# The last head of a cached-attention decode block: one accumulator bank cleared earlier, an output projection read in stored order, and small work moved into TensorE's waits

## Chip, cores, metric

One core of a Trainium2 chip runs the whole program. The metric is the device time of one execution in microseconds, as the median of several runs; a profiled run also gives the span (first to last instruction) and the granted TensorE clock.

## The reference

A modulated decode block with one token: a layernorm, attention of 32 query heads over a cache of 8 heads x 32768 keys x 128, an output projection, then a second layernorm and a two-layer ReLU network.

```python
mod = silu(c) @ w_mod                      # sa, ca, ga, sb, cb, gb, 512 each
h = layernorm(x) * (1 + ca) + sa
q = h @ wq                                 # 32 heads of 128
p = softmax(q . k_cache * 128**-0.5)       # 8 cache heads, 4 query heads each
o = p . v_cache
x = x + ga * (o @ wo)                      # wo: 4096 x 512
h = layernorm(x) * (1 + cb) + sb
x = x + gb * (relu(h @ w1) @ w2)           # 512 -> 1792 -> 512
```

The caches are 134 MB in bf16, all weights together 15 MB. Every byte is read once.

## The kernel before

One queue (SyncE) streams everything in a fixed order: w_mod, wq, the heads' K and V alternating, and at the end the last V (in three pieces), wo (four pieces), w1 (two), w2 (six). For each head, VectorE transposes K, TensorE multiplies it with a block-diagonal q (scores), ScalarE takes the exponential, VectorE transposes it, TensorE multiplies with V (`pv`, into `o_ps`, which VectorE must clear first). The order of TensorE's and VectorE's instructions is written by hand. Below, x1 is x after the first addition (`x1T` holds it as columns), hidT are the products with w1, and ffn those with w2. The parts that the change touches:

```python
def open_o(g):                              # clears the bank of head g's o
    o_tiles[g] = ps_o.tile([16, 4 * Dh], F32, tag="o", name="o_ps")
    nc.vector.memset(o_tiles[g][:], 0.0)
# blocks(g): Y <- o_ps, four VectorE steps.     o_cols(g): oT <- Y, TensorE ("column sums")
# normalise(g): oT * Linv, then its spread-out form oA, two VectorE steps; and at a part's end spread(i)
# spread(i): o2 <- oA, one TensorE product and a cast
def project(i):                             # o2 times part i of wo
    ...
    if i < WOROWS:                          # parts 0 and 1 (6 of 8 heads): rows, four strips of the array
        nc.tensor.matmul(
            a_rows[0][32*(r%4):32*(r%4)+1, :].rearrange("o (a ko m) -> o a ko m", a=4, ko=KT),
            lhsT=o2_tiles[i][:, r:r+1],
            rhs=wo_sb[:, r, :].rearrange("p (a m ko) -> p a ko m", a=4, ko=KT), ...)
    ...                                     # parts 2 and 3 (one head each): columns
def join_rows():                            # rows of parts 0 and 1 to columns
    aT = rows_sb("aT")[:, 0, :]
    nc.vector.transpose(out=aT, in_=a_rows[0])
    ...                                     # four small products into attnT_ps
def keep_clock(n): ...                      # n filler products of 128x512, result unused

# the end of the order (head 6 = LAST - 1, head 7 = LAST)
            pv(g, (2,), range(6, 16))
            pv(g, (3,))
            next(soft)                      # sum of the exponentials (TensorE)
            next(soft, None)                # its reciprocal (VectorE)
            open_o(LAST)
            a_rows.append(row_bank("a_ps"))
            blocks(g)
        pv(LAST, (0, 1))
        o_cols(LAST - 1)
        normalise(LAST - 1)                 # with spread(2)
        pv(LAST, (2,))
        pv(LAST, (3,))
        blocks(LAST)
        project(0)
        keep_clock(2)
        o_cols(LAST)
        keep_clock(2)
        normalise(LAST)                     # with spread(3)
        project(1)
        keep_clock(3)
        project(2)
        join_rows()
        keep_clock(4)
        project(3)
        ...                                 # x1T; layernorm between keep_clock(4) and keep_clock(4)
        ...                                 # hidT = w1 products, ReLU on ScalarE to hid_bd
        x1_rows = four_rows(x1T[:], "x1", nc.vector.tensor_copy)
        keep_clock(1)
        ...                                 # 56 ffn products with w2
        o_rows = ffn_ps * gb_rows; o_bf = o_rows + x1_rows      # VectorE, two steps
    nc.scalar.dma_start(out=out..., in_=o_bf[:])
```

## Time and profile before

| | before |
|---|---|
| median of the first 3 runs | 359.49 us (358.87 to 360.19) |
| span of the profiled run, granted clock | 358.0 us, 0.948 |
| HBM read | 149.42 MB, 417 GB/s over the span |
| TensorE, VectorE, ScalarE busy | 79%, 58%, 8% |

The busy shares tell little here: the kernel has a long stage paced by the stream, and a tail of 50 us in which single waits count. The tail is read from the timeline (start us, length us, engine, line, operation, output<-inputs, shapes, count, and in brackets the idle time before it with its releaser, that is, what ended the wait). PE are TensorE's products, PEld its weight loads, DVE is VectorE, ACT ScalarE; SPq and ACTq are the queues from which SyncE and ScalarE issue transfers. These rows of before mark its stages: the column sums of head 7, the first step on x1, the ffn, and the last two steps with the output's issue.

```profile
314.79 0.69 DVE L433 TENSOR_SCALAR_CACHE_REDUCE S_g<-S_ps 128x512 f32<-128x512 f32 x1 [2.92 <-PE S_ps L427]
...
341.85 0.38 PE L526 MATMUL acc_ps<-mask_sb,Y 16*128 16x4 f32 x2
...
346.94 0.16 DVE L690 TENSOR_TENSOR x1T<-acc_ps,modT_sb 128x4 f32<-128x4 f32 x1 [2.10 <-PE acc_ps L574]
...
351.77 3.29 PE L724 MATMUL ffn_ps<-w_sb,hid_bd 128*4 128x128 bf16 x56 [0.25 <-ACT hid_bd L709]
355.10 0.28 DVE L729 TENSOR_TENSOR o_rows<-ffn_ps,gb_rows 4x128 f32<-4x128 f32 x1 [3.26 <-PE ffn_ps L724]
...
355.73 0.55 ACTq L732 DMA_DIRECT2D out_dram<-o_bf  x1
```

The first row, the maximum over the last scores, lies before everything that the change touches. All stages below are given from its start, so that what happened earlier in a run doesn't enter. No wait in these rows names a transfer.

### The profile page before, as it was taken

How to read it: one execution, taken by the hardware profiler on the slowest of the kernel's cores; microseconds unless marked ns; L12 is line 12 of the kernel's file. 1: busy time of each engine (PE TensorE's matmuls, PEld its weight loads, DVE VectorE, ACT ScalarE, POOL GpSimd, SP SyncE). 2: the span in 40 equal slices, each digit the busy share in tenths (PEclk: the TensorE clock that was granted, in tenths of full speed). 3: DMA queues.
4: the chain of work that ended last, by engine and by line, in shares of the span. 5: the costliest groups of instructions: out<-in, count | busy, mean ns of one | idle time of the engine just before them, and what ended most of it. 6: DMA issues, size and time to landing. Idle time of an engine off the chain costs nothing. (4 is left out here: it accounts for less than half of the span.)

```text
span 358.0 us, 4070 instructions
## 1 busy us (share of the span) xinstructions
PE 281.7 (79%) x1351; PEld 114.3 (32%) x1354; DVE 207.7 (58%) x269; ACT 28.2 (8%) x68; POOL 8.5 (2%) x14
## 2 busy tenths in 40 slices
PE   0453681997998798879789798979597979989996
PEld 0121230333343334333333233323233333433445
DVE  8545775784677377463938095826855393832141
ACT  1121003001010101010100100010100010030000
POOL 9000000000000000000000000000000000000000
PEclk9996996799899999999969999999999896999999
DMA  8999999999999999999999999999999999999990
GB/s 324 434 443 432 416 448 425 436 439 421 445 425 432 439 425 445 421 432 436 432 443 423 428 439 429 437 430 421 443 432 432 439 419 443 428 421 428 419 398 14
DMA packets 7077, 149.61 MB, mean 418 GB/s; under 512 B 792, under 2 KB 1048, under 8 KB 2200
## 3 DMA queue, kind: packets, MB, share of 16 engines
q1 hardware_dynamic: 7056, 149.43, 97.3%
q8 instruction: 9, 0.15, 0.1%
q14 instruction: 4, 0.03, 0.0%
q10 hardware_dynamic: 8, 0.00, 0.0%
HBM read 149.42 MB, written 0.00 MB: 417 GB/s over the span
## 5 line engine op out<-in xcount | busy, mean ns | idle before, releaser
L407 DVE STREAM_TRANSPOSE KTt<-Ksb 128x2048 f32<-128x2048 f32 x64 | 143.3, 2284 | 68.5 <-DMA Ksb<-in_A_k_cache_dram 60.7
L489 PE MATMUL o_ps<-Vsb,PT_g 128*16 (+1 forms) x512 | 129.5, 393 | 22.4 <-ACT qbd L391 9.7
L427 PE MATMUL S_ps<-KTt,qbd 128*128 128x512 bf16 x512 | 123.0, 391 | 21.6 <-DVE KTt L407 20.2
L427 PEld LDWEIGHTS <-qbd 128*128 128x128 bf16 x512 | 49.0, 98 | 86.4 <-issue 28.6
L489 PEld LDWEIGHTS o_ps<-Vsb,PT_g 128*16 x416 | 37.2, 89 | 90.2 <-issue 63.9
L433 DVE TENSOR_SCALAR_CACHE_REDUCE S_g<-S_ps 128x512 f32<-128x512 f32 x16 | 11.0, 690 | 28.1 <-PE S_ps L427 28.1
L391 ACT COPY qbd<-qrep_sb 32x128 bf16<-32x128 bf16 x32 | 9.4, 295 | 138.2 <-PE S_ps L427 137.1
L470 DVE STREAM_TRANSPOSE PT_g<-P_g 128x1024 bf16<-128x1024 bf16 x8 | 9.7, 1218 | 6.6 <-ACT P_g L464 6.6
L489 PEld LDWEIGHTS <-PT_g 128*16 128x16 bf16 x96 | 8.4, 90 | 12.1 <-issue 0.8
L461 ACT ACTIVATE nbias<-Mb_ps 128x1 f32<-128x1 f32 x8 | 1.4, 171 | 133.3 <-PE Mb_ps L459 133.3
L233 PE MATMUL xc_ps<-cx_sel,cx_bd 16*128 16x2 bf16 x4 | 0.3, 172 | 12.8 <-DVE cx_bd L227 12.8
L464 ACT ACTIVATE P_g<-S_g,nbias 128x1024 bf16<-128x1024 f32 x8 | 9.2, 1148 | 0.2
L520 DVE SCALAR_TENSOR_TENSOR Y<-o_ps,smask,Y 16x128 f32<-16x128 f32 x24 | 8.1, 339 | 0.8
L179 DVE COPY sel<-ident_bf 128x128 bf16<-128x128 bf16 x4 | 7.6, 3731 | 0.0
L476 PE MATMUL L_ps<-Lexp,ones_f 128*128 128x4 f32 x16 | 3.1, 266 | 4.3 <-DVE Lexp L473 4.3
L518 DVE TENSOR_SCALAR Y<-o_ps,smask 16x128 f32<-16x128 f32 x8 | 2.2, 271 | 6.8 <-PE o_ps L489 6.8
L601 PE MATMUL spare_ps<-qbd,ident_bf 128*128 128x512 bf16 x19 | 5.4, 380 | 0.2 <-issue 0.2
L476 PEld LDWEIGHTS L_ps<-Lexp,ones_f 128*128 128x128 f32 x16 | 3.4, 239 | 6.0 <-issue 5.4
L445 PE MATMUL mT_ps<-ident_f,m_p 128*1 128x128 f32 x8 | 2.2, 270 | 3.9 <-DVE m_p L442 2.0
L539 DVE TENSOR_TENSOR oT_sb<-acc_ps,Linv 128x4 bf16<-128x4 f32 x8 | 1.2, 151 | 6.8 <-PE acc_ps L526 6.8
L448 DVE TENSOR_REDUCE Mrow<-mT_ps 1x4 f32<-1x128 f32 x8 | 2.1, 258 | 4.6 <-PE mT_ps L445 4.6
L510 DVE MEMSET o_ps<- 16x512 f32 x8 | 3.9, 485 | 0.8
(112 smaller groups left out, 86.1 us busy)
## 6 DMA issues: line engine op xcount, KB each, us to landing
Ksb<-in_A_k_cache_dram SPq DMA_DIRECT2D x16, 4096.0 KB, 28.8
Vsb<-in_A_v_cache_dram SPq DMA_DIRECT2D x15, 4096.0 KB, 25.1
wq_sb<-in_A_wq_dram SPq DMA_DIRECT2D x1, 4096.0 KB, 18.9
Vsb<-in_A_v_cache_dram SPq DMA_DIRECT2D x2, 2048.0 KB, 21.6
wm_sb<-in_w_mod_dram SPq DMA_DIRECT2D x1, 3072.0 KB, 10.4
wo_sb<-in_A_wo_dram SPq DMA_DIRECT2D x1, 2048.0 KB, 24.9
w_sb<-in_B_w_dram SPq DMA_DIRECT2D x1, 1344.0 KB
wo_sb<-in_A_wo_dram SPq DMA_DIRECT2D x1, 1024.0 KB, 26.8
```

Source lines behind the costliest of these rows:

```text
L179: nc.vector.tensor_copy(out=sel[:, hp, :].rearrange("p (a c) -> p a c", a=4), in_=src)
L391: nc.scalar.copy(out=o, in_=i)
L407: t = nc.vector.transpose(out=KTt[:].bitcast(F32), in_=Ksb[:, 32 * half:32 * half + 32, :].rearrange("p j d -> p (j d)").bitcast(F32),)
L427: nc.tensor.matmul(S_ps_tiles[g], lhsT=qbd[g % 2][:, hp, s, :], rhs=KTv[:, 16 * sl:16 * sl + 16, h, :, par], start=(t4 == 0 and sl == 0 an ...
L433: nc.vector.tensor_scalar(out=S_tiles[g][:, G, :], in0=S_ps_tiles[g], scalar1=1.0, scalar2=None, op0=ALU.mult, op1=ALU.max, accum_out=m_ti ...
L464: nc.scalar.activation(out=P_g[:], in_=S_g[:].rearrange("p g f -> p (g f)"), func=ACT.Exp, bias=nbias[:], scale=scale, accum_out=l_g[:],)
L470: nc.vector.transpose(out=PT_g[:], in_=P_g[:])
L476: nc.tensor.matmul(L_ps[:], lhsT=ones_f[:], rhs=Lexp[:], start=True, stop=True)
L489: nc.tensor.matmul(o_tiles[g][:], lhsT=PT, rhs=Vx, start=False, stop=False, skip_group_check=True)
L510: nc.vector.memset(o_tiles[g][:], 0.0)
L520: nc.vector.scalar_tensor_tensor(out=Y[:], in0=o[:, s], scalar=smask[:, s:s + 1], in1=Y[:], op0=ALU.mult, op1=ALU.add,)
L601: nc.tensor.matmul(spare[0], lhsT=ident_bf[:], rhs=qbd[0][:, 0, 0:4, :], start=True, stop=True)
```

## The change

The intent is to shorten TensorE's chain between the last head's softmax and the end: (1) clear the last head's o bank a softmax step sooner; (2) move the spread of head 6 to between the products with the third and fourth pieces of V; (3) read wo's rows as stored and let the VectorE transpose do the permutation; (4) put project(1) under head 7's normalisation and drop fillers; (5) compute x1's rows in the layernorm's wait instead of just ahead of the ffn; (6) issue the output from SyncE.

```diff
-def layernorm_T(src_T, stat_in, dst_T, shiftT, nscaleT, tagp):
+def layernorm_T(src_T, stat_in, dst_T, shiftT, nscaleT, tagp, meanwhile=None):
     ...                                        # statistics product, nu
+    if meanwhile:
+        meanwhile()
     ...
 # project, parts 0 and 1
-    a_rows[0][...].rearrange("o (a ko m) -> o a ko m", a=4, ko=KT), lhsT=o2_tiles[i][:, r:r + 1],
-    rhs=wo_sb[:, r, :].rearrange("p (a m ko) -> p a ko m", a=4, ko=KT), ...
+    a_rows[0][...], lhsT=o2_tiles[i][:, r:r + 1],
+    rhs=wo_sb[:, r, :], ...
 # join_rows
-    nc.vector.transpose(out=aT, in_=a_rows[0])
+    nc.vector.transpose(
+        out=aT.rearrange("p (a ko m) -> p a ko m", a=4, ko=KT),
+        in_=a_rows[0].rearrange("p (a m ko) -> p a ko m", a=4, ko=KT),
+    )
 # the order (normalise no longer spreads; in the loop spread follows normalise as before)
+            open_o(LAST)
             pv(g, (2,), range(6, 16))
             pv(g, (3,))
             next(soft)
             next(soft, None)
-            open_o(LAST)
 ...
         pv(LAST, (2,))
+        spread(2)
         pv(LAST, (3,))
 ...
         o_cols(LAST)
         keep_clock(2)
+        project(1)
         normalise(LAST)
-        project(1)
-        keep_clock(3)
+        spread(3)
+        keep_clock(2)
         project(2)
+        keep_clock(1)
         join_rows()
-        keep_clock(4)
+        keep_clock(2)
         project(3)
 ...
-        keep_clock(4)
-        layernorm_T(...)
-        keep_clock(4)
+        keep_clock(3)
+        layernorm_T(..., meanwhile)            # expansion of x1; keep_clock(2); row product; keep_clock(2)
+        x1_rows = const.tile([KT, P], F32)
+        nc.vector.tensor_copy(out=x1_rows[:], in_=x1_ps[0])
 ...
-        x1_rows = four_rows(x1T[:], "x1", nc.vector.tensor_copy)
         keep_clock(1)
 ...
-    nc.scalar.dma_start(out=out..., in_=o_bf[:])
+    nc.sync.dma_start(out=out..., in_=o_bf[:])
```

More of the change, by code (lines that the diff above doesn't have):

```diff
@@ L325, with expand @@
         )
-    def four_rows(src_T, name, copy):
+    def expand(src_T, name):
         e = const.tile([P, 32, KT], F32, name=f"{name}_exp")
@@ L333, in four_rows @@
         )
+        return e
+    def four_rows(e, name):
         r_ps = bank(f"{name}_ps")[0:KT, 0:P]
@@ L337, in four_rows @@
         )
-        rows = const.tile([KT, P], F32, name=f"{name}_rows")
-        copy(out=rows[:], in_=r_ps)
-        return rows
-    gb_rows = four_rows(modT_sb[:, 5 * KT:6 * KT], "gb", nc.scalar.copy)
+        return r_ps
+    gb_rows = const.tile([KT, P], F32)
+    nc.scalar.copy(out=gb_rows[:], in_=four_rows(expand(modT_sb[:, 5 * KT:6 * KT], "gb"), "gb"))
     hT = const.tile([P, KT], BF16)
@@ L545, in normalise @@
         PT_tiles.pop(g)
-        if g == sum(WOP[i]) - 1:
-            spread(i)
     o2_tiles = {}
@@ L568, in project @@
                 nc.tensor.matmul(
-                    a_rows[0][32 * (r % 4):32 * (r % 4) + 1, :].rearrange("o (a ko m) -> o a ko m", a=4, ko=KT), lhsT=o2_tiles[i][:, r:r + 1],
-                    rhs=wo_sb[:, r, :].rearrange("p (a m ko) -> p a ko m", a=4, ko=KT), start=False, stop=(i == WOROWS - 1 and r >= n - 4), skip_group_check=True,
+                    a_rows[0][32 * (r % 4):32 * (r % 4) + 1, :], lhsT=o2_tiles[i][:, r:r + 1],
+                    rhs=wo_sb[:, r, :], start=False, stop=(i == WOROWS - 1 and r >= n - 4), skip_group_check=True,
                 )
@@ L638 @@
                 normalise(g - 1)
+                if g in [sum(w) for w in WOP]:
+                    spread(part_of(g - 1))
             if soft:
@@ L694, with meanwhile @@
         h2T = const.tile([P, KT], BF16)
-        keep_clock(4)
-        layernorm_T(x1T[:], stat2, h2T[:], modT_sb[:, 3 * KT:4 * KT], ncb[:], "ln2")
-        keep_clock(4)
+        x1_ps = []
+        def meanwhile():
+            e = expand(x1T[:], "x1")
+            keep_clock(2)
+            x1_ps.append(four_rows(e, "x1"))
+            keep_clock(2)
+        keep_clock(3)
+        layernorm_T(x1T[:], stat2, h2T[:], modT_sb[:, 3 * KT:4 * KT], ncb[:], "ln2", meanwhile)
+        x1_rows = const.tile([KT, P], F32)
+        nc.vector.tensor_copy(out=x1_rows[:], in_=x1_ps[0])
         for part, (k0, k1) in enumerate(W1P):
@@ L731 @@
         nc.vector.tensor_tensor(out=o_bf[:], in0=o_rows[:], in1=x1_rows[:], op=ALU.add)
-    nc.scalar.dma_start(out=out[0, 0].rearrange("(i n) -> i n", i=KT), in_=o_bf[:])
+    nc.sync.dma_start(out=out[0, 0].rearrange("(i n) -> i n", i=KT), in_=o_bf[:])
 _INS = ['A_x', 'A_k_cache', 'A_v_cache', 'A_wq', 'A_wo', 'B_x', 'B_w1', 'B_w2', 'c', 'w_mod']
```

## The prediction

> **What bounds the kernel now.** I read the occupancy by slices first, then the chain that ended last, then the timeline of the last 60 us, because the diff touches nothing before the last head but a rewritten helper. Occupancy by slices (engine, then 40 digits of 8.95 us each):
>
> ```profile
> PE   0453681997998798879789798979597979989996
> ...
> DMA  8999999999999999999999999999999999999990
> ```
>
> The transfers are saturated until the last slice: 149 MB at 417 GB/s is 358 us by itself, so up to the arrival of the last head's K the stream sets the pace. The table of stretches shows where the stream ends (columns: stretch, PE, PEld, DVE, ACT, POOL, granted clock, share of the DMA engines, GB/s):
>
> ```profile
> 349.00:350.00 1.00, 0.76 (x23) 0.64 (x23) 0.39 (x2) 0.00 (x0) 0.00 (x0) 1.00 0.33 116
> 350.00:351.00 1.00, 1.00 (x39) 0.88 (x37) 0.00 (x0) 0.00 (x0) 0.00 (x0) 1.00 0.01 2
> ```
>
> The data are in at about 349.5 us, but the span ends at 358.0. The end is therefore TensorE's in-order queue with its waits, and the chain names it (start us, length us, what):
>
> ```profile
> 323.25 0.33 PE L_ps L476 x2
> ...
> 323.61 0.18 DVE Linv L479
> ...
> 323.88 0.50 DVE o_ps L510
> ...
> 324.42 7.07 PE o_ps L489 x32
> 331.49 0.33 PE acc_ps L526 x2
> ...
> 332.03 0.30 DVE oA L540
> ...
> 332.38 0.18 PE o_ps L555
> 332.56 6.57 PE o_ps L489 x30
> ...
> 339.56 1.82 PE a_ps L568 x12
> ...
> 341.92 0.31 PE acc_ps L526 x2
> ...
> 342.99 1.00 PE a_ps L568 x8
> ...
> 346.39 0.51 PE acc_ps L574 x16
> ```
>
> The reader is to see three things. TensorE, done with the sum at 323.58, stands until 324.42 because VectorE clears the last head's o only after the reciprocal. It stands again from 331.81 to 332.56, as the spread of head 6 waits for two VectorE steps. And the products with wo's rows are slow for their size, as two rows of the per-line view show (min/median/max ns):
>
> ```profile
> L364 PE MATMUL q_ps<-wq_sb,hT x32: 376/379/380, 21.6 to 23.4; 128*1 128x512 bf16 x32
> ...
> L568 PE MATMUL a_ps<-wo_sb,o_sb x24: 609/630/642, 338.8 to 343.4; 128*1 128x512 bf16 x24
> ```
>
> Both are 1x512 products in four strips of the array; one reads runs of 32 neighbours, the other every fourth element. By the timeline q's last 28 take 1.68 us (0.060 each), wo's 8 at 342.99 take 1.00 us (0.125 each).
>
> **What the Trainium skill says.** "TensorE: Matmul & The Clock Gate", section "Back-to-back issue gap": a warm N=512 matmul costs N/2.4 + 2.5 ns, about 216 ns. The trace has 7.07/32 = 0.221 us: agrees. So keep_clock's fillers cost about 0.22 us each (four take 0.97 us here). "SBUF — State Buffer", section "Door 1: The DMA port swizzle", has a note on 16-byte lines, by which bf16 may be strided up to 8 elements before full bandwidth is lost. A step of 4 elements should then be free; the two rows above say it is not, for four strips at once, and I follow the trace. "DMA: Bandwidth & Descriptors", section "Issuing engines are not separate DMA queues": another issuing engine saves only issue time. The trace has 0.55 us for the output's issue from ScalarE and 0.28 to 0.36 us for the equally small loads from SyncE.
>
> **The change, part by part.** The order of instructions of the built kernels gives each move.
>
> (1) The clearing of o for the last head now stands before the reciprocal, behind Lexp (done at 320.4). It finishes near 321, under head 6's products. The 32 products of head 7 can start at 323.6 instead of 324.42: **-0.84**.
>
> (2) The spread of head 6 moves from before 32 products to between the two 16s. The gap 331.81 to 332.56 (0.75) goes; the spread's own work, 0.1 to 0.18, stays: **-0.6**.
>
> (3) wo's rows are read as stored. At q's rate, 16 products take 0.96 instead of 2.0, and 8 take 0.48 instead of 1.0. For project(0) the path is a race: from the last product of head 7 (339.56) VectorE needs 1.5 us for Y (ready 341.07), while TensorE reaches the column sums only at 341.92, after project(0) and two fillers. Now project(0) and two fillers take 0.96 + 0.44 = 1.4, so Y sets it, at about +1.55 instead of +2.36: **-0.8**.
>
> (4) From the end of those column sums (342.23) to the end of project(3) (346.91) were 4.68 us. New order: two fillers and project(1) 0.44 + 0.48, under which oT and oA (0.54) hide; spread 0.1 to 0.15; two fillers 0.44; project(2) 0.51; one filler 0.22; join 0.17 to 0.2; two fillers 0.44; project(3) 0.51; sum 3.4 to 3.5, so **-1.2**. Of this, about 0.5 is the faster project(1), about 0.45 the wait hidden behind it, and 0.2 or so one filler fewer. Against it: the VectorE transpose of wo's rows, 0.72 us contiguous, now reads PSUM in steps of four. It starts after the cast of o2 (about +1.45) and would end at +2.2, just before join at +2.3, so there is no slack. The start-up shows a penalty for reductions of 128 SBUF elements read with a step: 0.36 against 0.27 us. Scaled to 512 elements (an estimate; that this carries over to PSUM is assumed) it is +0.36, of which 0.25 lands on the path: **+0.25**.
>
> (5) Layernorm: one filler fewer before the statistics (they waited for VectorE until 347.57 anyway), x1's expansion (0.28 on VectorE) lies in the wait from 347.60 to 347.99, and x1's row product (about 0.38) among the four fillers, before h2T at 349.18. I count **0**. After hidT, the row product no longer stands before the first ffn product, which came 0.16 after ScalarE had finished: **-0.14**.
>
> (6) Output issued from SyncE: **-0.2**.
>
> Sum: -0.84 - 0.6 - 0.8 - 1.2 + 0.25 - 0.14 - 0.2 = -3.5. From 359.5: **356.0 us**.
>
> **Rivals.** (a) The transfers become the wait. The last piece of w2 was issued at 341.6 and takes at least 8.8 us, so it lands near 350.4. The first ffn product moves from 351.77 to about 348.4 (the sum without the output), and the last piece's four products of 0.059 us are wanted at about 351.4: 1.0 us to spare. wo's first piece lands at 311.9 + 24.9 = 336.8 and is wanted at 338.1; the third, issued about 312.8, lands near 340.8 and is wanted at about 341.4. All hidden, but with 0.6 to 1.3 us to spare. If one binds, the gain shrinks to about 2.5: 357.0. (b) The strided transpose takes twice as long: join waits some 0.7 more than in my contiguous count, 356.5. (c) The step is not why wo's products are slow: (3) and 0.5 of (4) vanish, gain 2.2: 357.3. Against it stands that the same form runs at 0.060 per product on q, at full clock. (d) Fewer fillers let the clock fall: at half rate the last 10 us cost some 4 more, 360. The granted clock reads 1.00 throughout the tail, and no gap that I foresee is over 0.5 us. Unlikely. A gain of 2% (7.2 us) is out of reach: with the data in at 350.4, then 0.2 of products, 0.6 of VectorE and 2.3 for the output, the span can't fall under about 353.5, which is 4.5 saved.
>
> **Range and chances.** The parts carry plus or minus 0.7 together; the before runs alone spread 358.87 to 360.19. Rivals (a) to (c) lie on the slow side, so the range is 355.1 to 357.8. Within 2% means 352.3 to 366.7: 0.98. Faster 0.01, slower 0.01.
>
> **What would show it.** Step 1: no idle time of TensorE before head 7's first product, VectorE's clear ahead of the reciprocal. Step 2: head 7's second 32 products follow the column sums within 0.1 us. Step 3: wo's row products at 379 ns each, 0.06 apart; column sums released by Y, not by a filler. Step 4: 3.4 to 3.8 us from column sums to the end of project(3); the transpose's mean near 1 us. Step 5: 2.3 us from x1T to the first hidT product as before; ffn starts within 0.1 of ScalarE's end. Step 6: about 2.1 us from o_bf to the end, not 2.3. I am wrong if TensorE is seen to wait for w1, w2 or wo, or if the granted clock falls below 1.00 in the tail.

## The result

| | before | after |
|---|---|---|
| median, 6 runs each | 359.19 us (358.62 to 360.19) | 355.58 us (355.43 to 357.48) |
| ratio, 95% interval | | 0.9906 (0.9881 to 0.9931) |
| span of the profiled run | 358.0 us | 353.7 us |

A ratio is the mean time of one kernel's runs over that of the other's of the same rounds, so it is not quite the ratio of the two medians. The gain is 3.6 us by the medians and 3.4 by the ratio. The two spans differ by more, 4.3 us, and the profile shows why that isn't all the change's doing.

The occupancy by slices of after (same engines as shown of before, one slice is 8.84 us):

```profile
PE   0352781999898979897969797979789787989995
...
DMA  8999999999999999999999999999999999999994
```

The last slice, which for before read 0 in the DMA row, now reads 4: the stream runs into the final slice. The chain that ended last is short, and mostly made of transfers (start us, length us, what):

```profile
305.94 25.65 DMA Vsb<-in_A_v_cache_dram
...
331.61 16.67 DMA w_sb<-in_B_w_dram
...
348.32 2.41 PE ffn_ps L742 x40
...
350.75 0.29 DVE o_rows L747
```

In before the chain went through TensorE's products from 307.6 us on. Here it goes from the ffn back to a landing of w2 at 348.28, and from there to V. The timeline of after has the rows that answer to those of before:

```profile
313.42 0.69 DVE L437 TENSOR_SCALAR_CACHE_REDUCE S_g<-S_ps 128x512 f32<-128x512 f32 x1 [1.99 <-PE S_ps L431]
...
338.27 0.38 PE L530 MATMUL acc_ps<-mask_sb,Y 16*128 16x4 f32 x2
...
340.15 0.61 PEld L576 LDWEIGHTS <-wo_sb 128*128 128x128 bf16 x16 [0.36 <-DMA wo_sb<-in_A_wo_dram]
...
342.33 0.16 DVE L700 TENSOR_TENSOR x1T<-acc_ps,modT_sb 128x4 f32<-128x4 f32 x1 [1.60 <-PE acc_ps L576]
...
348.32 2.39 PE L742 MATMUL ffn_ps<-w_sb,hid_bd 128*4 128x128 bf16 x40 [0.15 <-DMA w_sb<-in_B_w_dram]
350.75 0.28 DVE L747 TENSOR_TENSOR o_rows<-ffn_ps,gb_rows 4x128 f32<-4x128 f32 x1 [5.98 <-PE ffn_ps L742]
```

Two readings. First, waits for transfers (wo, then w2) stand in the tail, which before had none. Second, the maximum over the last scores already starts 1.37 us earlier than in before (313.42 against 314.79), ahead of anything that was changed. The table of stretches explains that (stretch, PE, PEld, DVE, ACT, POOL busy, granted clock, DMA share, GB/s); before, then after:

```profile
296.00:298.00 2.00, 2.00 (x7) 0.98 (x5) 0.46 (x3) 0.00 (x0) 0.00 (x0) 0.50 0.91 393
```

```profile
296.00:298.00 2.00, 1.23 (x9) 0.69 (x7) 0.87 (x4) 0.00 (x0) 0.00 (x0) 1.00 0.83 360
```

In the profiled run of before the clock was granted at half for these 2 us and for the next 4, and head 6's products with V started 0.43 us apart; in that of after it was at 1.00, and they took 0.25 us each. Whether this belongs to the kernels or to the single run had to be tried.

Two facts of the change itself, from the per-line view (min/median/max ns) of wo's row products and of the transpose, after:

```profile
L570 PE MATMUL a_ps<-wo_sb,o_sb x24: 376/378/379, 336.6 to 339.3; 128*1 128x512 bf16 x24
...
L588 DVE STREAM_TRANSPOSE aT<-a_ps x1: 707/707/707, 339.9 to 339.9; 128x512 f32<-128x512 f32 x1
```

The row products went from 630 to 378 ns. The transpose, which now reads PSUM in steps of four, takes 0.707 us; contiguous it took 0.717 in before.

### The profile page after: what moved, and what is told of

Read it like the earlier page. It is cut to its first block, busy times and chain, and to the rows that moved or that the text cites. A ratio compares the mean times of both kernels' runs of the same rounds, so it can differ in the third digit from the quotient of the medians.

```text
span 353.7 us, 4064 instructions
## 1 busy us (share of the span) xinstructions
PE 278.1 (79%) x1348; PEld 111.8 (32%) x1351; DVE 207.3 (59%) x269; ACT 28.2 (8%) x68; POOL 8.5 (2%) x14
## 5 line engine op out<-in xcount | busy, mean ns | idle before, releaser
L493 PE MATMUL o_ps<-Vsb,PT_g 128*16 (+1 forms) x512 | 128.0, 382 | 22.4 <-ACT qbd L395 9.5
L493 PEld LDWEIGHTS o_ps<-Vsb,PT_g 128*16 x416 | 35.9, 86 | 90.7 <-issue 66.4
```

The costliest lines, as they stand in the source:

```text
L493: nc.tensor.matmul(o_tiles[g][:], lhsT=PT, rhs=Vx, start=False, stop=False, skip_group_check=True)
```

## The experiments

Theory A: the change shortens TensorE's chain by about 3.4 us, as summed in the prediction, but its new end lies within half a microsecond of what the stream allows, so that part of the gain is turned into waits for transfers whenever the clock is up before the last scores. Theory B: TensorE's chain still sets the end, and the waits for transfers in the profile of after are incidental. A third question is what the clock does. The runs went out in four groups (before_again, p1, p3, u6; the three x and u3; after_again, u7, n1_one_op_end; n1_out_act). A group shared a chip and its runs of before, so ratios are compared across groups, and spans and stages only with their scatter in mind.

All times in one table first (span: median of the listed runs, with the lowest and highest; last column: start of the first of the last VectorE steps, from the maximum over the last scores, in the profiled run; for the two kernels with one step at the end it is that step).

| run | ratio to before (95%) | span, us | chain, us |
|---|---|---|---|
| before (first profile) | | 358.0 (one run) | 40.31 |
| after (first profile) | 0.9906 (0.9881 to 0.9931) | 353.7 (353.5 to 354.3) | 37.33 |
| before_again | 1.0018 (0.9995 to 1.0041) | 358.0 (356.6 to 358.5) | 41.91 |
| p1_open_o | 0.9978 (0.9956 to 1.0001) | 356.2 (355.6 to 356.9) | 39.38 |
| p3_rows | 0.9961 (0.9939 to 0.9983) | 355.5 (355.3 to 356.8) | 39.08 |
| u6_out_act | 0.9915 (0.9896 to 0.9935) | 354.0 (353.7 to 354.5) | 36.91 |
| x_after_late | 0.9962 (0.9940 to 0.9984) | 355.9 (355.0 to 356.5) | 39.84 |
| x_before_late | 1.0002 (0.9980 to 1.0025) | 357.5 (356.6 to 358.7) | 41.91 |
| x_after_less | 0.9902 (0.9881 to 0.9924) | 353.3 (353.0 to 354.4) | 36.90 |
| u3_rows_strided | 0.9941 (0.9913 to 0.9969) | 354.4 (354.4 to 356.0) | 38.10 |
| after_again | 0.9914 (0.9894 to 0.9934) | 353.8 (353.6 to 354.8) | 36.89 |
| u7_no_fillers | 0.9948 (0.9927 to 0.9970) | 355.4 (354.6 to 356.0) | 38.91 |
| n1_one_op_end | 0.9896 (0.9875 to 0.9916) | 353.4 (353.4 to 353.6) | 37.36 |
| n1_out_act | 0.9913 (0.9894 to 0.9933) | 354.0 (353.4 to 354.1) | 36.91 |

All kernels passed the comparison with the reference. x_after_less did too, though it uses wrong data for a quarter of one cache head's V on purpose, so its pass says nothing about its result. Steps 2, 4 and 5 were not run alone; what they gave is read from the stages of the traces.

### before_again: the kernel before, unchanged

No edit.

> The kernel before, unchanged, as a second profile and a measure of the noise. Ratio 1.000 within 0.003 on either theory. If the clock theory holds (the first profile of before had the granted clock at 0.50 from about 294.6 to 302 us, where the one of after had 1.00, and this put the last score product at 314.77 instead of 313.40 us), the end of the scores of head 7 will vary from run to run of the same kernel by about 1.4 us with the clock in that stretch, and the span of before with it.

Measured: ratio 1.0018, within the noise. Its spans run from 356.6 to 358.5, those of the eleven runs of before beside it from 356.3 to 358.2. The new profile has the clock at 1.00 from 284 to 312 us, and the maximum over the last scores starts at 313.70 instead of 314.79. So the early start in the profile of after was the clock's, not the change's. All fourteen profiles bear this out: the four with half clock from 296 to 302 us (before, after_again, u6_out_act, n1_out_act) have the maximum at 314.57 to 314.89, the ten others at 313.42 to 313.86. But this run wasn't short (358.5), for another reason (timeline, then stretches):

```profile
350.66 4.91 PE L724 MATMUL ffn_ps<-w_sb,hid_bd 128*4 128x128 bf16 x56 [0.25 <-ACT hid_bd L709]
```

```profile
350.50:351.00 0.50, 0.34 (x5) 0.34 (x6) 0.23 (x1) 0.00 (x0) 0.00 (x0) 0.76 0.00 0
351.00:352.00 1.00, 1.00 (x12) 1.00 (x11) 0.00 (x0) 0.00 (x0) 0.00 (x0) 0.50 0.00 0
...
354.00:354.50 0.50, 0.50 (x10) 0.50 (x8) 0.00 (x0) 0.00 (x0) 0.00 (x0) 0.82 0.12 33
```

The 56 ffn products took 4.91 us instead of 3.29, because the clock was at half from about 350.8 to 354.2 (worked out from the two mixed stretches). Every stage up to the ffn agrees with the first profile within 0.03 us: column sums at 27.04 against 27.06 us after the maximum, x1 at 32.12 against 32.15, ffn at 36.96 against 36.98. So the stages, counted from the last scores, are reproducible to a few hundredths; what sets the two profiles of before apart is the clock, in two places. That the clock also makes the scatter of 2 us among the unprofiled runs is likely, but not shown.

### p1_open_o: step 1 alone

```diff
             next(soft)
             next(soft)
+            open_o(LAST)
             pv(g, (2,), range(6, 16))
             pv(g, (3,))
             next(soft)
             next(soft, None)
-            open_o(LAST)
```

> Before plus step 1 alone (the clearing of the last head's o a softmax step sooner). By the prediction: TensorE's wait before head 7's first product falls from 0.84 us to about 0, so -0.84 us (ratio 0.9977). Rival (the clearing is hidden or another wait takes its place): the wait stays over 0.4 us, or the later chain gives it back, ratio 1.000.

Measured: TensorE no longer waits ahead of head 7's products (timeline):

```profile
322.14 7.07 PE L489 MATMUL o_ps<-Vsb,PT_g 128*16 128x512 bf16 x32
```

The first of them comes at 8.70 us after the maximum instead of 9.63, -0.93, and the last steps at 39.38 instead of 40.31, again -0.93: nothing gives it back. Timing: 0.9978, which is -0.8 us, with an interval that just reaches 1.

### p3_rows: step 3 alone

```diff
-    a_rows[0][...].rearrange("o (a ko m) -> o a ko m", a=4, ko=KT), lhsT=o2_tiles[i][:, r:r + 1],
-    rhs=wo_sb[:, r, :].rearrange("p (a m ko) -> p a ko m", a=4, ko=KT), ...
+    a_rows[0][...], lhsT=o2_tiles[i][:, r:r + 1],
+    rhs=wo_sb[:, r, :], ...
-    nc.vector.transpose(out=aT, in_=a_rows[0])
+    nc.vector.transpose(out=aT as "p a ko m", in_=a_rows[0] read as "p (a m ko) -> p a ko m")
```

> Before plus step 3 alone (wo's rows read as stored, the transpose permutes). By the prediction: products 379 ns each and 0.06 us apart instead of 627 ns and 0.125; -0.8 us at the column sums and -0.5 in project(1), so -1.3 us (ratio 0.9964), with the transpose at about 0.71 us as in the profile of after. Rival: the column sums are held by Y and the transpose, so that the faster products only lengthen waits: 0 to -0.5 us.

Measured: column sums at 26.33 us instead of 27.06 (-0.73), x1 at 30.92 instead of 32.15 (-1.23, so another -0.50 in project(1)), the end at -1.23. The timeline shows that Y, not TensorE, now releases the column sums:

```profile
339.95 0.38 PE L526 MATMUL acc_ps<-mask_sb,Y 16*128 16x4 f32 x2 [0.15 <-DVE Y L520]
```

The products took 377 ns each, the transpose 0.72 us. Timing: 0.9961, which is -1.4 us, clear of 1. This also settles rival (c) of the prediction: the step of four was the only thing changed about the products' reading, and it is what made them slow.

### u6_out_act: step 6 undone

```diff
-    nc.sync.dma_start(out=out..., in_=o_bf[:])
+    nc.scalar.dma_start(out=out..., in_=o_bf[:])
```

> After with step 6 alone undone (output issued from ScalarE again). By the prediction +0.2 us (end of the last VectorE step to end of span 2.36 -> about 2.56). By the two profiles (2.36 us with SyncE, 2.30 with ScalarE) no difference: 0 +- 0.05 us in the profile, ratio to after 1.000.

Measured: from the end of the last step (352.18) to the end of the span (354.5) 2.3 us, as in before. This profile had half clock before the last scores (maximum at 314.68), and no wait of TensorE in its tail names a transfer, so it shows the chain of after without waits for transfers: last steps at 36.91 us, where the first profile of after had 37.33. The ratio, 0.9915 on another chip than after's 0.9906, doesn't tell 0 from 0.2 us; the ends of all fourteen profiles, under n1_out_act below, do.

### x_after_late and x_before_late: 512 KB more in the stream

```diff
+    elif kind == "extra":
+        t = piece("w12_sb", KT * Dff + FT * D, 4 * D).rearrange("p (a b d) -> p a b d", a=2, b=FB)
+        src = w2_v[:, 0:2, :]
 ...
+    stream += [("extra",)]
     stream += [("w1", i) for i in range(len(W1P))] + ...
```

> After with one more transfer of 512 KB (data that nothing reads) in the stream just ahead of w1, so that w1 and w2 land 1.2 us later (0.52 MB at 0.42 MB/us). Theory A (in after the transfers set the end whenever the clock stays up): the first hidden product waits for w1 and the span grows by 0.8 to 1.2 us. Theory B (TensorE's chain still sets the end; the waits on transfers in the profile of after, 0.7 us in all, are incidental): 0 to +0.3 us.

> Before with the same additional 512 KB. Both theories: no change (ratio 1.000 within 0.002), as w1 and w2 land more than 2 us ahead of their first products there. If it grows, the transfer also costs time in another way (for instance slower V or wo), and x_after_late must be read against it.

Measured: before doesn't notice (1.0002). After grows from a median span of 353.8 (after_again, on another chip) to 355.9, by 1.4 us in the lowest spans (353.6 and 355.0). The timeline of the late after:

```profile
346.17 0.50 PE L725 MATMUL hidT_ps<-h2T,w_sb 128*128 128x1 bf16 x14 [1.24 <-DMA w_sb<-in_B_w_dram]
...
348.64 4.80 PE L746 MATMUL ffn_ps<-w_sb,hid_bd 128*4 128x128 bf16 x56 [0.25 <-ACT hid_bd L732]
```

The wait for w1 is 1.24 us, just the additional transfer's 0.52 MB at 0.42 MB/us. So after, with the clock up before the last scores, had no slack left against w1, and before had at least 1.2 us. That is theory A. The growth beyond 1.2 us was not expected by either: the clock was at half from about 348.4 us, and the ffn took 4.80 us. That the wait brought this about isn't shown, as the ffn of x_before_late met half clock too (4.91 us), with no wait for a transfer ahead of it.

### x_after_less: 2 MB fewer ahead of wo

```diff
-    stream += [("v", LAST, (0, 1)), ("v", LAST, (2,)), ("v", LAST, (3,))] + ...
+    stream += [("v", LAST, (0, 1)), ("v", LAST, (2,))] + ...
 # in pv
+    if g == LAST and us[0] == 3:
+        loaded[("v", g, 3)] = need(("v", g, 2))
```

> After without the last 2 MB piece of V (its products read the third piece a second time: a wrong result on purpose), so that wo, w1 and w2 land some 5 us sooner. Theory A: TensorE's waits for wo, w1 and w2 are gone and the span falls by 0.3 to 0.6 us where the clock stays up, 0.1 to 0.4 us in the median. Theory B: no change. In either case the chain from the end of the scores to the first ffn product takes 33.6 us or less (33.69 in the profile of after).

Measured: no wait of TensorE names wo, w1 or w2 any more (timeline), and the last steps come at 36.90 us after the maximum instead of 37.33.

```profile
347.19 3.29 PE L744 MATMUL ffn_ps<-w_sb,hid_bd 128*4 128x128 bf16 x56 [0.20 <-ACT hid_bd L730]
```

The profiles of after's order agree on this: the two with such waits and nothing added (after, n1_one_op_end) have a chain of 37.33 and 37.36 us, the four without (after_again, u6_out_act, x_after_less, n1_out_act) one of 36.89 to 36.91. So the waits for transfers cost about 0.4 us of chain, and theory B's "no change" is refuted by the profiles. The times fit but would not do alone: the lowest span is 353.0, against 353.5 and 353.6 for after, on other chips, and the intervals of the ratios (0.9902 against 0.9906 and 0.9914) overlap. The chain to the first ffn product is 33.57 us, as expected.

### u3_rows_strided: step 3 undone in after

The edit is the reverse of p3_rows.

> After with step 3 alone undone (wo's rows read with a step of four, plain transpose). By steps 3 and 4 of the prediction TensorE's chain is 0.75 + 0.5 = 1.2 to 1.3 us longer up to x1T. Theory A: only part of it shows in the span, +0.7 to +1.0, because after's chain waited for transfers. Theory B: the whole +1.2 to +1.3.

Measured: the chain is 38.10 us against 36.89 without waits (+1.21), but the span of four runs of six is 354.4 against after's lowest of 353.5 and 353.6, on other chips: +0.8 to +0.9. Its tail has no waits for transfers. By the spans, part of the 1.2 us of step 3 is thus not seen in after, because the transfers stand there instead. By the ratios (0.9941 against 0.9914 and 0.9906) step 3 is worth 1.0 to 1.3 us, and these don't tell the two theories apart. Two runs of six took 355.6 and 356.0; only profiles would tell whether the clock did that.

### after_again: the kernel after, unchanged

No edit.

> After, unchanged, against before on another chip, with more rounds. If the gain is what the stages of the traces add up to (3.4 us on TensorE's chain, of which about 0.4 is given to waits for transfers while the clock stays up), the lowest spans of the two kernels differ by 2.7 to 3.0 us and the means by 3.0 to 3.6 (ratio 0.990 to 0.992).

Measured: ratio 0.9914 against eleven runs of before on the same chip, -3.1 us. The lowest spans are 353.6 and 356.5, 2.9 apart. This profile fell in the half-clock case before the last scores (maximum at 314.89, as late as in the first profile of before), so the two can be laid side by side stage by stage. Its chain, where after's first profile had only transfers:

```profile
339.35 0.35 DVE Y L524
...
339.74 0.38 PE acc_ps L530 x2
...
342.25 0.24 PE spare_ps L606
342.49 0.18 PE acc_ps L593 x8
...
348.41 0.04 issue
348.46 3.30 PE ffn_ps L742 x56
```

Y leads to the column sums; the join (8 products at 342.49) follows the filler at once, so the transpose isn't on the path; the ffn follows ScalarE by 0.04 us.

### u7_no_fillers: the tail without its fillers

```diff
     def keep_clock(n):
         ...
-        for _ in range(n):
+        for _ in range(0 * n):
```

> After without any of the filler products of the tail. If they hold the clock up (rival d of the prediction), the granted clock falls to 0.50 in the last 10 us and the ffn products take 4.9 us instead of 3.3: +1 to +3 us. If they only take up TensorE's time, the chain shortens but the transfers hold the end: 0 to -0.3 us.

Measured: the median span grows by 1.6 us (355.4 against 353.8). The clock and the ffn (stretches, then timeline):

```profile
338.00:340.00 2.00, 1.09 (x11) 0.57 (x11) 1.01 (x5) 0.00 (x0) 0.00 (x0) 1.00 1.08 445
...
341.00:342.00 1.00, 0.56 (x23) 0.50 (x16) 0.00 (x0) 0.00 (x0) 0.00 (x0) 0.52 1.06 452
```

```profile
347.04 5.29 PE L742 MATMUL ffn_ps<-w_sb,hid_bd 128*4 128x128 bf16 x56 [0.66 <-DMA w_sb<-in_B_w_dram]
```

The clock is at half from 341 on. The single wait of TensorE before that is at most 0.63 us; it was busy 1.9 of the 3 us from 338 to 341. Four of the six runs have a mean clock of 0.927 to 0.933 and spans of 355.2 to 356.0, the other two 0.942 and 0.952 and spans of 354.6 and 354.8. The first ffn product comes at 347.04, hardly earlier than with the fillers (347.11), and waits for w1 and w2 stand ahead of it. So where the transfers set the end the fillers cost nothing, and without them the clock fell. In after_again, whose chain has no wait for transfers, about 3.8 us of the chain are fillers; what fewer of them would give in such a run wasn't tried.

### n1_one_op_end and n1_out_act: a shorter end

If the stream sets the end, only what follows the last landing is left to shorten. The last step adds x1's rows to the product with gb. TensorE can add x1/gb beforehand, in the same bank:

```diff
+    gbinv = const.tile([P, KT], F32)                       # at the start
+    nc.vector.reciprocal(out=gbinv[:], in_=modT_sb[:, 5 * KT:6 * KT])
+    place_g = expand(gbinv[:], "pg")
 # in meanwhile: e = x1T * place_g, and
+    nc.tensor.matmul(ffn_ps, lhsT=rowpick[:], rhs=e[...], start=True, stop=False, ...)
 # ffn products accumulate onto it (start=False)
-    nc.vector.tensor_tensor(out=o_rows[:], in0=ffn_ps, in1=gb_rows[:], op=ALU.mult)
-    nc.vector.tensor_tensor(out=o_bf[:], in0=o_rows[:], in1=x1_rows[:], op=ALU.add)
+    nc.vector.tensor_tensor(out=o_bf[:], in0=ffn_ps, in1=gb_rows[:], op=ALU.mult)
```

> After with the last two VectorE steps made one: x1/gb is added by TensorE into the sum of the ffn (its row product writes there first, from an expansion scaled with 1/gb, built at the start), so that one product with gb ends the kernel. After the last landing nothing but one step (0.28 us and a hand-over) goes: -0.3 us whatever holds the stream before it (span 353.4 where after has 353.7).

Measured: 355.21 us (355.16 to 355.46), ratio 0.9896, span 353.4 in four of five runs: -0.3 us against after's median of 353.7, the best kernel. The result is correct for these inputs; an element of gb that is exactly zero would give a division by zero, so for general use this needs a guard. One step is left after the ffn (timeline):

```profile
350.92 0.28 DVE L754 TENSOR_TENSOR o_bf<-ffn_ps,gb_rows 4x128 bf16<-4x128 f32 x1 [6.18 <-PE ffn_ps L749]
```

The same with the output issued from ScalarE:

> The kernel with one step at the end, with its output issued from ScalarE instead of SyncE; chosen because its spans hardly spread (353.4 four times, 353.6 once). By step 6 of the prediction the span grows by 0.2 us (353.6). If the shorter issue is hidden behind the output's landing, as the profiles of after and of after with the issue moved back suggest (2.2 to 2.4 us from the last step to the end on both engines), it stays 353.4.

Measured: 353.4 twice and 354.0 to 354.1 four times. The profiled run was one of 354.0, and it had the clock at half from 296 to 302 us, with the maximum over the last scores at 314.57 us instead of the 313.56 of n1_one_op_end; the other three of the four weren't profiled. The two early ones equal the 353.4 with SyncE; that the other four are slower by the clock alone is shown for one of them. Independent of the clock is the stretch from the end of the last VectorE step to the end of the span: 2.20 to 2.36 us in the seven profiles with SyncE, 2.24 to 2.34 in the seven with ScalarE. The shorter issue (0.29 instead of 0.55 us) is not seen there.

## Why the prediction was right, point by point

The chain of after without waits for transfers (after_again) against the first profile of before, both with the same clock history:

| step | predicted | measured, by stage |
|---|---|---|
| 1 clearing | -0.84 | -0.92: first product of head 7 at 8.71 instead of 9.63 (p1 alone: -0.93) |
| 2 spread | -0.6 | -0.53: end of head 7's products at 23.32 instead of 24.77, less step 1 |
| 3 column sums | -0.8 | -0.76: from there to the column sums 1.53 instead of 2.29 |
| 4 to x1 | -1.2 + 0.25 | -1.08: 4.01 instead of 5.09 |
| 5 to the last steps | -0.14 | -0.13: 8.03 instead of 8.16 |
| 6 output | -0.2 | 0: 2.2 to 2.4 us from the last step to the end on both engines |
| sum | -3.5 | -3.4 |

- Steps 1 to 3: right in mechanism and nearly in size. Y sets the column sums, 1.53 us after head 7's last product; the prediction said 1.55.
- Step 4: the -1.2 was -1.08. The +0.25 for the strided transpose was wrong: its scaling from short reductions in SBUF to a transpose from PSUM doesn't hold, the transpose takes 0.71 us either way. The two errors partly cancel. Of the 1.08, p3 shows 0.50 from faster products in project(1); the rest, about 0.6, is the order and the dropped fillers, which were not tried apart. Two slips stand in the prediction's working of this step: its terms add up to 3.3 to 3.4 us, not 3.4 to 3.5, and the new order has two fillers fewer after the column sums (seven instead of nine), not one. From the end of the column sums to the end of project(3) after_again took 3.58 us.
- Step 5: right; x1T to the first hidden product takes 2.29 us as before, and the ffn starts 0.04 us after ScalarE.
- Step 6: wrong. The saved issue time doesn't reach the end; why it doesn't was not tried.
- That the sum comes out within 0.1 us is in part luck: the 0.2 us of step 6 that did not come are made up by 0.08 more in step 1 and 0.13 more in step 4.
- The prediction counts 0.22 us for a filler from a formula of the Trainium skill ("TensorE: Matmul & The Clock Gate", "Back-to-back issue gap"), which gives it for an isolated product; for a stream with weight loads the same section has about 131 ns. Head 7's 32 products, each with its weight load, took 0.221 us apiece, so here the formula holds and the 131 ns do not.
- Rival (a), transfers become the wait: the prediction gave it 0.6 to 1.3 us of slack. It came in part: where the clock was up before the last scores, TensorE's chain began 1.1 to 1.4 us earlier than in the profile that the slack had been counted from, while the stream ended when it had before (DMA share from 349 to 350 us 0.35 in after, 0.33 in before), and this used the slack up. The cost is 0.44 us of chain (37.33 against 36.89), of which 0.32 lies in the ffn, at the second of w2's six pieces, after 16 of 56 products; the prediction had looked at the last piece only. x_after_late shows no slack left.
- Rival (b): refuted by the 0.707 us. Rival (c): refuted by p3.
- Rival (d), the clock: called unlikely, and it didn't hit after as it stands in any of its profiles. But the mechanism is live: it hit before's ffn in two profiles (4.91 us), after's when it was made to wait, and after's without fillers.
- The statement that I would be wrong if TensorE were seen to wait for w1, w2 or wo went too far: it did wait, for 0.44 us of chain, and the measured time still came out near the sum. A 3.0 us gain of chain (40.31 to 37.33) is what the first two profiles show, not 3.4; how the states of the clock make up for this in the mean was neither predicted nor shown.

What stays open: how much of the mean gain is the chain and how much is that after's tail loses the clock less often. With half clock before the last scores the chain gives 3.4 us (before against after_again, in the spans as well: 358.0 and 354.6), with the clock up there and in before's ffn 3.0 (40.31 against 37.33). The lowest spans differ by 2.8 to 2.9 us and the ratios give 3.1 to 3.4; profiles of only one run each can't say how often each case occurs.

## What to carry to other kernels

Count a tail's stages from the last event ahead of the change; they repeat to a few hundredths of a microsecond while the spans scatter by two. Before summing gains on one engine's chain, ask how far the next limit is in the run where everything earlier goes well, not in the one profile at hand. And give a permutation to the instruction that doesn't pay for it: here the transpose read with a step for nothing, where the matmuls in four concurrent strips took about double (eight of them 1.00 us of the chain in before, 0.53 in after_again).

## What the Trainium skill lacked or had wrong

- "SBUF — State Buffer", "Door 1: The DMA port swizzle", the note on 16-byte lines: bf16 may be strided up to 8 elements before full bandwidth is lost. A moving operand read with a step of 4, in four column strips at once, took 630 ns per 1x512 product, and eight of them 1.00 us of the chain; read in order 378 ns and 0.53 us. One strip alone wasn't tried.
- No page found gives the cost of a VectorE transpose from PSUM read with a step: 128x512 f32 with a step of 4 took 0.707 us, contiguous 0.717.
- "TensorE: Matmul & The Clock Gate", Part 1, has the clock at half after at least one idle window of about 3.4 us. The length agrees (half clock from about 350.8 to 354.2 us in before_again), but 3.4 us without work were not needed: without fillers it halved at 341 us with TensorE busy for 1.9 of the 3 us ahead and no wait of its products over 0.63 us, and in before_again after 3.4 us of which it was busy for 2.75, with none over 0.41 us. Part 1 also tells of a kernel that lost the clock by short, frequent idles, but not how much idle that takes.
- "DMA: Bandwidth & Descriptors", "Issuing engines are not separate DMA queues", speaks of transfers started on several engines at once, which save the sequencer's issue time. It says nothing of a single output moved to an engine that issues it faster: 0.29 us of issue on SyncE against 0.55 on ScalarE, and 2.20 to 2.36 against 2.24 to 2.34 us from the last step to the end, so nothing was saved.
